# A fused block-sparse attention and gMLP kernel: first batch in two query halves, loads and weights reordered

## Chip, cores and metric

One core of a Trainium2 chip. The metric is the device time of one execution in microseconds (us). The kernel before takes 223.69 us, the median of 6 runs (223.38 to 223.85). All times within an execution are read from one profiled execution.

## The reference, cut to what matters

Four batches, 8 heads, 768 positions, head size 64. Attention with a block mask (blocks of 32: the neighbours, the first and last block row and column, and three sampled blocks per row), then a gated MLP with a spatial product over the positions.

```python
scores = np.where(mask, scale * q @ k.T, -1e9)          # per batch and head, 768 x 768
attn = softmax(scores);  x = concat_heads(attn @ v)      # x: 4 x 768 x 512
h = relu(x @ w_in);  u, v = h[..., :512], h[..., 512:]   # w_in: 512 x 1024
v_n = (v - mean(v)) / sqrt(var(v) + 1e-6)
v_s = einsum('ts,bsd->btd', w_spatial, v_n) + b_spatial  # w_spatial: 768 x 768
out = (u * v_s) @ w_out                                  # w_out: 512 x 512
```

## The kernel before, in words

The order of all instructions is written out by hand, and each engine executes its own in that order. Heads come in pairs: pair p holds two heads, four pairs make a batch, and there are 16 pairs. The main loop (L483 on) runs over p and 12 steps s; a step is called a slot here and numbered g = 12p + s, so that a batch has 48 slots and a head six.

A slot holds these parts:

- qk_exp (L285): two matmuls of 384 columns on TensorE (PE) give one 128-row chunk of keys against all 768 queries, in one of two PSUM tiles (ps, tag sc). ScalarE (ACT) takes their exponential (L294) into the tile a_all. The mask is added by the same matmul: rows 64 to 87 of the tiles kt and qt hold 24 block indicators and mask values. These tiles are filled once for head slot 0 and copied on VectorE (DVE) to slots 1 to 3 (mask_rows, L260 to 262); head j uses slot j % 4.
- av (L299), seven slots behind: six matmuls of 65 columns for a chunk of 128 queries. After six chunks, norm (L313) divides by the row sums (reciprocal L319, product L320) into xn. When both heads of a pair are done, xn is transposed to xt, by PE (L323) or by a DMA (L343).
- Matmuls of the gMLP of the batch before. moe_units (L362) makes 108 of them for a batch, each of 512 columns (L386): 48 for h, 36 for the spatial product, 24 for the output. They are added in slot 56 of the batch that follows and drawn from slot 57 on, spread over 48 slots. In the h part the order is v0 v1 v2 u0 v3 u1 v4 u2 v5 u3 u4 u5 (row chunks of the v and u halves; four matmuls each). A chunk of v gets its relu and statistics on DVE (on ACT in the last batch), and after three of them GpSimd (POOL) computes rstd (L403, L405). A chunk of u gets its relu on ACT (L415) and issues the normalization of the chunk of v before it (L409). The last batch's gMLP mostly runs after all attention.

The loads of q, k and v (L91) go through SyncE's queue (SP) into fp32 tiles st_q, st_k and st_v of two buffers each. POOL casts them to bf16 (prepare, L116; cast_v, L111; L109 and L112). Heads 0 and 1 are cast by halves, by DVE and ACT, and transposed one by one (tr_head, L225; copies L220). Pairs 1 to 5 are transposed by PE (tr_pair, L234, with DVE copies L244), later ones by DMA (tr_dma, L271, then split_pair, L276). PE's transposes and the gMLP share two PSUM buffers of tag moe. The weights are loaded in nine pieces (L138) into fp32 staging tiles that borrow buffers of gMLP tiles, and cast on POOL (L150): w_in in slots 7 and 19, w_spatial in slot 55, w_out in slot 79. w_spatial is transposed by six DMAs in slots 60 to 78 (wspt, L348). Loops over keep_warm (L178) are matmuls without use, at the start.

Of the kernel before, what the change touches and what calls it, by code (L numbers as in the profile page):

```python
# [26 lines left out]
def kernel(  # L27
# [16 lines left out]
    nc = tc.nc  # L44
# [29 lines left out]
    b_col = const.tile([128, NCH], FP32)  # L74
    mhalf = const.tile([128, NCH], FP32)

    qt = [const.tile([KR, S], BF16, name=f"qt{s}") for s in range(4)]
    kt = [const.tile([KR, S], BF16, name=f"kt{s}") for s in range(4)]
    vv = [const.tile([128, 2, NCH, VA], BF16, name=f"vv{s}") for s in range(3)]


    st = {}
# [1 line left out]
    def dram(src, b, h0, nh):  # L84
        return src[b, h0:h0 + nh].rearrange("h (p c) d -> p h (c d)", c=NCH)

    def st_tile(p, nm):
        st[nm, p] = work.tile([128, 2, NCH * D], FP32, tag=f"st_{nm}", bufs=2, name=f"st_{nm}")
        return st[nm, p]

    def load(p, names="qkv", eng=nc.sync):  # L91
        b, g = divmod(p, NG)
        for nm, src in (("q", q), ("k", k), ("v", v)):
            if nm in names:
                eng.dma_start(out=st_tile(p, nm), in_=dram(src, b, 2 * g, 2))

    nat = {}

    def nat_tile(p, nm):
        nat[nm, p] = work.tile([128, NCH, 2, D], BF16, tag=f"nat_{nm}", bufs=2,  # L100
                               name=f"nat_{nm}")
# [8 lines left out]

    def cast_v(p):  # L111
        nc.gpsimd.tensor_copy(  # L112
            out=vv[p % 3][:, :, :, 0:D],
            in_=st.pop(("v", p)).rearrange("p h (c d) -> p h c d", d=D))

    def prepare(p):  # L116
        for nm in "kq":
            nat_tile(p, nm)
            cast_qk(p, nm, slice(0, 2), nc.gpsimd)
        cast_v(p)  # L120

# [9 lines left out]
        w_pieces.append((moe_w_out.rearrange("(g p) f -> p g f", p=128)[:, 2 * g:2 * g + 2],  # L133
                         w_out_t[:, 2 * g:2 * g + 2, :]))
    w_staged = deque()
    w_tags = deque(["un", "vsb", "vn", "gn", "gt"])

    def load_weights(n):  # L138
        for _ in range(n):
# [19 lines left out]
    nc.sync.dma_start(out=samp_i, in_=_listify(sampled_blocks).bitcast(I32))  # L159
    for h in range(2):  # L160
        nc.sync.dma_start(out=stq[:, h:h + 1], in_=dram(q, 0, h, 1))
    load(0, "v", nc.sync)
    load(1, "qkv", nc.sync)
    nc.sync.dma_start(out=b_col, in_=moe_b_spatial.rearrange("(p c) -> p c", c=NCH))

    ind_nat = const.tile([NB, S], BF16)
    ind = const.tile([NB, S], BF16)
# [28 lines left out]
                            base=0, pattern=[[-1, NB], [0, BLK]], channel_multiplier=1)  # L196
    make_identity(nc, ident)

    for s in range(3):
        nc.gpsimd.memset(vv[s][:, :, :, D:VA], 1.0)  # L200
    nc.gpsimd.memset(mhalf, -0.5)

# [31 lines left out]
    def tr_pair(p, nm, third):  # L234
        if third == 0:
            tr_ps[nm] = psum.tile([128, S], BF16, tag="moe", bufs=2, name="ps_tr")
        src, ps = nat[nm, p], tr_ps[nm]
        for c in (2 * third, 2 * third + 1):
            nc.tensor.transpose(out=ps[:, c * 128:(c + 1) * 128],  # L239
                                in_=src[:, c].rearrange("p h d -> p (h d)"), identity=ident)  # L240
        if third == 2:
            nat.pop((nm, p))
            for h in range(2):
                nc.vector.tensor_copy(out=(qt if nm == "q" else kt)[(2 * p + h) % 4][0:D, :],  # L244
                                      in_=ps[h * D:(h + 1) * D, :])

    tr_head(0, "k", dve_copy)
# [9 lines left out]
    tr_head(0, "q", dve_copy)  # L257
    keep_warm(8, 128)

    def mask_rows(sl):  # L260
        nc.vector.tensor_copy(out=kt[sl][D:KR, :], in_=kt[0][D:KR, :])
        nc.vector.tensor_copy(out=qt[sl][D:KR, :], in_=qt[0][D:KR, :])

    def second_head():
        mask_rows(1)
        cast_qk(0, "k", slice(1, 2), nc.vector)
        cast_qk(0, "q", slice(1, 2), nc.vector)

    tt = {}

    def tr_dma(p, nm):  # L271
# [4 lines left out]
    def split_pair(p, nm):  # L276
        src = tt.pop((nm, p)).rearrange("x c n -> x (c n)")
        for h in range(2):
            nc.vector.tensor_copy(out=(qt if nm == "q" else kt)[(2 * p + h) % 4][0:D, :],  # L279
                                  in_=src[h * D:(h + 1) * D, :])  # L280


# [2 lines left out]
    def qk_exp(j, ci):  # L285
        if ci == 0:
            a_ref[j] = work.tile([128, NCH, S], BF16, tag="a_all", bufs=3, name="a_all")
        ps = psum.tile([128, 1024], FP32, tag="sc", bufs=2)
        for hf in range(2):
            nc.tensor.matmul(out=ps[:, hf * 512:hf * 512 + HALF],  # L290
                             lhsT=kt[j % 4][:, ci * 128:(ci + 1) * 128],
                             rhs=qt[j % 4][:, hf * HALF:(hf + 1) * HALF],
                             start=True, stop=True)
        nc.scalar.activation(  # L294
            out=a_ref[j][:, ci, :].rearrange("p (b c) -> p b c", b=2),
            in_=ps.rearrange("p (b c) -> p b c", b=2)[:, :, 0:HALF],
            func=AF.Exp, scale=0.125)

    def av(j, qc):  # L299
        if qc == 0:  # L300
            av_ref[j] = psum.tile([128, 512], FP32, tag="av", bufs=2,
                                  name="ps_av")[:, 0:NCH * VA].rearrange(
                                      "p (c d) -> p c d", d=VA)
        p, h = divmod(j, 2)
        for ci in range(NCH):
            nc.tensor.matmul(out=av_ref[j][:, qc, :],  # L306
                             lhsT=a_ref[j][:, ci, qc * 128:(qc + 1) * 128],
                             rhs=vv[p % 3][:, h, ci, :],
                             start=(ci == 0), stop=(ci == NCH - 1))
        if qc == NCH - 1:  # L310
            a_ref.pop(j)

    def norm(j):  # L313
        p, h = divmod(j, 2)
# [47 lines left out]
    def moe_units(b):  # L362
# [3 lines left out]
        vsb = work.tile([128, NCH, DH], BF16, tag="vsb", bufs=2)  # L366
        vn = work.tile([128, NCH, DH], BF16, tag="vn", bufs=2)
        gn = work.tile([128, NCH, DH], BF16, tag="gn", bufs=2)
        gt = work.tile([128, NCH, NDH, 128], BF16, tag="gt", bufs=2)
        mv = work.tile([128, NCH, 2], FP32, tag="mv", bufs=2)  # L370
        std = work.tile([128, NCH], FP32, tag="std", bufs=2)
        rstd = work.tile([128, NCH], FP32, tag="rstd", bufs=2)
# [48 lines left out]
        def in_proj(tcc, cols, post):  # L421
            add(NDM, lambda g: (xt(g)[:, tcc * 128:(tcc + 1) * 128], w_in_t[:, g, cols]),
                lambda ps: post(tcc, ps))

        for i in range(NCH + 2):
            if i < NCH:
                in_proj(i, slice(DH, DFF), v_post)
            if i >= 2:
                in_proj(i - 2, slice(0, DH), u_post)

        def g_tr(tcc):
            ps = psum.tile([128, S], BF16, tag="moe", bufs=2, name="ps_g")
# [39 lines left out]
    slots_left = 0  # L472
    LAG = 7

    for p in range(NP + 1):
        for s in range(12):
            g = 12 * p + s
            j, ci = divmod(g, NCH)
            if p == NP and g - LAG >= 2 * NP * NCH:
                break  # L480
            if p < NP:
                qk_exp(j, ci)
            if p == 0 and s == 0:  # L483
                second_head()
            if p == 0 and s < 6:
                keep_warm(2, 128)
            if p == 0 and s == 3:
                tr_head(1, "k", dve_copy)
            if p == 0 and s == 4:
                tr_head(1, "q", dve_copy)  # L490
                mask_rows(2)
                mask_rows(3)
            if p <= NG:
                first = 0 if p else 6
                if first <= s < first + 3:
                    tr_pair(p + 1, "k", s - first)
                elif first + 3 <= s < first + 6:
                    tr_pair(p + 1, "q", s - first - 3)
            elif p + 1 < NP and s in (5, 9):
                split_pair(p + 1, "k" if s == 5 else "q")  # L500
            if s == 10 and NG + 1 < p + 2 < NP:
                tr_dma(p + 2, "k")
                tr_dma(p + 2, "q")
            if p == 0 and s == 0:
                cast_v(0)
                prepare(1)
                load(2)
                load_weights(2)
            if s == 7 and p + 2 < NP:
                if p + 3 < NP:  # L510
                    load(p + 3)
                if p in (0, 3, 4, 5):
                    load_weights((2, 0, 0, 2, 1, 2)[p])
                prepare(p + 2)
                if p in (0, 1, 4, 6):
                    cast_weights((2, 2, 0, 0, 3, 0, 2)[p])
            if moe_q and slots_left > 0:
                budget += len(moe_q) / slots_left
                slots_left -= 1
                while moe_q and budget >= 0.5:  # L520
                    moe_q.popleft()()
                    budget -= 1
            if g >= LAG:
                ja, qc = divmod(g - LAG, NCH)
                av(ja, qc)
                if qc == NCH - 1:
                    norm(ja)
            if p in (NG + 1, NG + 2) and s in (0, 3, 6):
                wspt(3 * (p - NG - 1) + s // 3)
            if 1 <= p < NG and 8 <= s < 11:  # L530
                xtr_third(p - 1, s - 8)
            if s == 8 and p >= NG:
                xtr(p - 1)
                if p % NG == 0:
                    moe_q.extend(moe_units(p // NG - 1))
                    slots_left = 48 if p < NP - NG else 52
                    budget = 0.0
# [34 lines left out]
```

The softmax here doesn't subtract the row's maximum and nothing guards it: scores larger than these inputs give would overflow.

## Time and profile before

| | |
|---|---|
| median of 6 runs | 223.69 us |
| the profiled execution | 223.13 us |
| its span, first to last instruction | 221.4 us |
| PE busy | 214.2 us (97%) |
| ACT busy | 177.1 us (80%) |
| DVE busy | 128.2 us (58%) |
| POOL busy | 64.1 us (29%) |
| the 192 exps (L294), one | 814 ns |
| mean granted TensorE clock | 0.997 |

The span is shorter than the execution's time by what lies around the program. "a<-b" names the tile written and those read. The mean duration of an instruction is longer than its share of an engine's time where the next one begins before it ends; the distance between starts is then the cost. A note such as [0.42 <-PE ps L290] says that the engine was idle for 0.42 us until that instruction of PE was done. A q after an engine's name is its queue.

### The profile page before, as it was taken

The numbers are of one execution on the slowest core, as the hardware profiler recorded it, in microseconds if no ns is written. First come the engines' busy times: TensorE is split into PE (matmuls) and PEld (weight loads), VectorE is DVE, ScalarE is ACT, GpSimd is POOL, SyncE is SP. The second block draws the span as 40 slices with busy tenths as digits, with TensorE's granted clock in tenths as the row PEclk, the third lists the DMA queues.
The fourth block names the chain that finished last, engine by engine and source line by source line (L and its number), as shares of the span: only waits on it lengthen the run. The fifth ranks groups of instructions, "written<-read, shape, count | busy, mean of one in ns | idle before, by whom it ended". The sixth has DMA issues, their size and how long they took to land.

```text
span 221.4 us, 5325 instructions
## 1 busy us (share of the span) xinstructions
PE 214.2 (97%) x2154; PEld 129.8 (59%) x2154; DVE 128.2 (58%) x282; ACT 177.1 (80%) x246; POOL 64.1 (29%) x88
## 2 busy tenths in 40 slices
PE   7999999999999999999999999999999999999993
PEld 3567777676565656566565656566656665544541
DVE  5656445467868455368777544378674433676531
ACT  5699999998899888888899878888989884265351
POOL 5436770439905701210607101210501000022000
PEclk9999999999999999999999999999999999999998
DMA  6779999995899877999674397998141114610015
GB/s 193 234 278 384 387 307 332 340 142 64 254 280 135 263 106 210 196 316 277 209 172 144 78 104 225 180 318 244 30 80 36 38 40 89 229 73 0 0 61 225
DMA packets 56092, 40.25 MB, mean 182 GB/s; under 512 B 39300, under 2 KB 51588, under 8 KB 56068
## 3 DMA queue, kind: packets, MB, share of 16 engines
q1 hardware_dynamic: 55780, 39.53, 68.1%
q10 hardware_dynamic: 288, 0.39, 0.6%
q8 instruction: 16, 0.26, 0.5%
q14 instruction: 8, 0.07, 0.1%
HBM read 24.38 MB, written 6.29 MB: 139 GB/s over the span
## 4 chain that ended last, share of the span: by engine, by line
PE 81%; ACT 14%; DVE 2%; issue 1%; POOLq 0%; POOL 0%
PE ps_moe L386 31%; PE ps L290 23%; ACT a_all L294 13%; PE ps_av L306 13%; PE ps_t L386 6%; PE ps_sc L386 3%; PE wps L180 2%; PE ps L228 1%; PE ps_x L330 1%; PE ps_g L434 1%; POOLq L567 0%; DVE gn L441 0%; DVE stats L399 0%; PE ps_tr L239 0%; ACT vsb L394 0%
## 5 line engine op out<-in xcount | busy, mean ns | idle before, releaser
L294 ACT ACTIVATE a_all<-ps 128x768 bf16<-128x768 f32 x192 | 149.5, 814 | 19.3 <-PE ps L290 10.7
L290 PE MATMUL ps<-qt,kt 88*128 88x384 bf16 x384 | 93.7, 325 | 1.8 <-ACT a_all L294 0.6
L306 PEld LDWEIGHTS <-a_all 128*128 128x128 bf16 x1152 | 60.4, 97 | 37.0 <-issue 0.4
L306 PE MATMUL ps_av<-vv,a_all 128*128 128x65 bf16 x1152 | 67.9, 194 | 0.0
L386 PE MATMUL ps_moe<-w_in_t,xt 128*128 128x512 bf16 x144 | 42.1, 378 | 0.0
L386 PE MATMUL ps_moe<-vn,w_spt 128*128 128x512 bf16 x108 | 31.8, 379 | 0.0
L290 PEld LDWEIGHTS <-kt 88*128 88x128 bf16 x384 | 28.2, 97 | 4.7 <-issue 1.9
L386 PEld LDWEIGHTS <-xt 128*128 128x128 bf16 x192 | 18.6, 97 | 16.1 <-issue 0.3
L112 POOL CAST vv<-st_v 128x768 bf16<-128x768 f32 x16 | 13.4, 837 | 45.8 <-PE ps_av L306 42.6
L441 DVE SCALAR_TENSOR_TENSOR gn<-ps_moe,b_col,un 128x512 bf16<-128x512 f32 x18 | 13.5, 749 | 18.6 <-PE ps_moe L386 18.5
L403 POOL TENSOR_SCALAR std<-mv 128x3 f32<-128x3 f32 x8 | 2.2, 278 | 72.2 <-DVE mv L400 59.5
L386 PE MATMUL ps_moe<-w_out_t,gt 128*128 128x512 bf16 x72 | 20.6, 379 | 0.1
L386 PEld LDWEIGHTS <-w_spt 128*128 128x128 bf16 x144 | 13.7, 97 | 11.4 <-issue 0.9
L399 DVE BATCH_NORM_STATS2 stats<-vsb 128x6 f32<-128x512 bf16 x24 | 16.7, 694 | 3.3 <-ACT vsb L394 2.7
L320 DVE TENSOR_TENSOR xn<-ps_av,rc 128x384 bf16<-128x384 f32 x32 | 17.8, 558 | 1.1
L396 DVE TENSOR_SCALAR vsb<-ps_moe 128x512 bf16<-128x512 f32 x18 | 12.4, 690 | 10.3 <-PE ps_moe L386 10.3
L109 POOL CAST nat_k<-st_k 128x768 bf16<-128x768 f32 x15 | 12.4, 824 | 17.5 <-DMA st_k<-in_k_dram 8.8
L319 DVE RECIPROCAL rc<-ps_av 128x6 f32<-128x6 f32 x32 | 6.0, 188 | 15.7 <-PE ps_av L306 15.6
L386 PEld LDWEIGHTS <-gt 128*128 128x128 bf16 x96 | 8.8, 97 | 6.9
L109 POOL CAST nat_q<-st_q 128x768 bf16<-128x768 f32 x15 | 12.5, 833 | 0.0
L279 DVE COPY kt<-tt_k 64x768 bf16<-64x768 bf16 x20 | 8.5, 424 | 6.2 <-DMA tt_k<-nat_k 6.0
L409 DVE TENSOR_SCALAR vn<-vsb,mv,rstd 128x512 bf16<-128x512 bf16 x24 | 10.3, 447 | 2.6 <-POOL rstd L405 2.5
(80 smaller groups left out, 172.4 us busy)
## 6 DMA issues: line engine op xcount, KB each, us to landing
st_v<-in_v_dram SPq DMA_DIRECT2D x16, 384.0 KB, 5.7
out_dram<-osb SPq DMA_DIRECT2D x24, 256.0 KB, 2.6
st_q<-in_q_dram SPq DMA_DIRECT2D x15, 384.0 KB, 3.7
st_k<-in_k_dram SPq DMA_DIRECT2D x15, 384.0 KB, 4.7
wst<-in_moe_w_spatial_dram SPq DMA_DIRECT2D x3, 768.0 KB, 8.2
wst<-in_moe_w_in_dram SPq DMA_DIRECT2D x4, 512.0 KB, 8.5
wst<-in_moe_w_out_dram SPq DMA_DIRECT2D x2, 512.0 KB, 6.9
st_k<-in_k_dram ACTq DMA_DIRECT2D x2, 192.0 KB, 3.0
```

The costliest lines, as they stand in the source:

```text
L109: eng.tensor_copy(out=dst, in_=src)
L112: nc.gpsimd.tensor_copy(out=vv[p % 3][:, :, :, 0:D], in_=st.pop(("v", p)).rearrange("p h (c d) -> p h c d", d=D))
L279: nc.vector.tensor_copy(out=(qt if nm == "q" else kt)[(2 * p + h) % 4][0:D, :], in_=src[h * D:(h + 1) * D, :])
L290: nc.tensor.matmul(out=ps[:, hf * 512:hf * 512 + HALF], lhsT=kt[j % 4][:, ci * 128:(ci + 1) * 128], rhs=qt[j % 4][:, hf * HALF:(hf + 1) * ...
L294: nc.scalar.activation(out=a_ref[j][:, ci, :].rearrange("p (b c) -> p b c", b=2), in_=ps.rearrange("p (b c) -> p b c", b=2)[:, :, 0:HALF], ...
L306: nc.tensor.matmul(out=av_ref[j][:, qc, :], lhsT=a_ref[j][:, ci, qc * 128:(qc + 1) * 128], rhs=vv[p % 3][:, h, ci, :], start=(ci == 0), st ...
L320: nc.vector.tensor_tensor(out=xn_ref[p][:, :, h, :], in0=ps[:, :, 0:D], in1=rc.to_broadcast([128, NCH, D]), op=ALU.mult)
L386: nc.tensor.matmul(out=box[0], lhsT=lhs, rhs=rhs, start=(i == 0), stop=(i == n - 1))
L396: nc.vector.tensor_scalar(out=vsb[:, tcc, :], in0=ps, scalar1=0.0, scalar2=None, op0=ALU.max)
L399: nc.vector.bn_stats(out=stats, in_=vsb[:, tcc, :])
L409: nc.vector.tensor_scalar(out=vn[:, tcc, :], in0=vsb[:, tcc, :], scalar1=mv[:, tcc, 0:1], scalar2=rstd[:, tcc:tcc + 1], op0=ALU.subtract, ...
L441: nc.vector.scalar_tensor_tensor(out=gn[:, tcc, :], in0=ps, scalar=b_col[:, tcc:tcc + 1], in1=un[:, tcc, :], op0=ALU.add, op1=ALU.mult)
```

## The change

The first batch gets a loop of its own of 48 slots. It goes over all eight heads for queries 0 to 383, three slots a head, and then over them again for queries 384 to 767. A slot computes two chunks of keys for 384 queries (qk_exp_half) and one chunk of queries of av_half, four slots behind. xtr_half transposes half a pair's xn on PE. There are eight head slots of kt and qt, in one tile each; head j uses slot j % 8. The mask rows are copied by DVE to slots 1 to 3 and by two DMAs to slots 4 to 7. Loads are issued in the order k1 q1 v0 k2 q2 v1, the mask rows, k3 q3 v2, two pieces of w_in, v3, two pieces of w_in. vv has four buffers, gt one.

Batch 0's first 16 gMLP matmuls (v0 v1 u0 v2) are drawn in slots 31 to 34 and 43 to 46, two in each; the other 92 from slot 55 on over 50 slots. w_spatial is loaded in slot 8 and cast in slots 34 and 38, and transposed in slots 45 to 55. The order of v and u chunks differs by batch. The core of the diff:

```diff
-    qt = [const.tile([KR, S], BF16, name=f"qt{s}") for s in range(4)]
-    kt = [const.tile([KR, S], BF16, name=f"kt{s}") for s in range(4)]
-    vv = [const.tile([128, 2, NCH, VA], BF16, name=f"vv{s}") for s in range(3)]
+    qt_all = const.tile([KR, H, S], BF16)
+    kt_all = const.tile([KR, H, S], BF16)
+    qt = [qt_all[:, h] for h in range(H)]
+    kt = [kt_all[:, h] for h in range(H)]
+    vv = [const.tile([128, 2, NCH, VA], BF16, name=f"vv{s}") for s in range(NG)]
...
-    load(0, "v", nc.sync)
-    load(1, "qkv", nc.sync)
-    nc.sync.dma_start(out=b_col, in_=moe_b_spatial.rearrange("(p c) -> p c", c=NCH))
+    load(1, "kq")
+    load(0, "v")
...
+    def qk_exp_half(g):
+        gh, i = divmod(g, NCH // 2)
+        grp, j = divmod(gh, H)
...
+        ps = psum.tile([128, 1024], FP32, tag="sc", bufs=2)
+        for u in range(2):
+            ci = 2 * i + u
+            nc.tensor.matmul(out=ps[:, u * 512:u * 512 + HALF],
+                             lhsT=kt[j][:, ci * 128:(ci + 1) * 128],
+                             rhs=qt[j][:, grp * HALF:(grp + 1) * HALF],
+                             start=True, stop=True)
+        nc.scalar.activation(out=a_ref["half", gh][:, 2 * i:2 * i + 2, :],
+                             in_=ps.rearrange("p (b c) -> p b c", b=2)[:, :, 0:HALF],
+                             func=AF.Exp, scale=0.125)
...
-        gt = work.tile([128, NCH, NDH, 128], BF16, tag="gt", bufs=2)
+        gt = work.tile([128, NCH, NDH, 128], BF16, tag="gt", bufs=1)
...
+        order = ("v0 v1 u0 v2 u1 u2 v3 v4 u3 v5 u4 u5" if b == 0 else
+                 "v0 v1 v2 v3 v4 v5 u0 u1 u2 u3 u4 u5" if last else
+                 "v0 v1 u0 v2 u1 v3 u2 v4 u3 v5 u4 u5")
...
+    LAG0 = 4
+    N0 = H * NCH
+
+    cast_qk(0, "k", slice(1, 2), nc.vector)
+    cast_qk(0, "q", slice(1, 2), nc.scalar)
+    prepare(1, "kq")
+    cast_v(0)
+    def mask_rows(h):
+        for t in (kt, qt):
+            nc.vector.tensor_copy(out=t[h][D:KR, :], in_=t[0][D:KR, :])
+
+    mask_rows(1)
+    load(2, "kq")
+    load(1, "v")
+    for t in (kt_all, qt_all):
+        nc.sync.dma_start(out=t[D:KR, 4:H, :],
+                          in_=t[D:KR, 0:1, :].to_broadcast([NB, H - 4, S]))
+    load(3, "kq")
+    load(2, "v")
+    load_weights(2)
+    load(3, "v")
+    load_weights(2)
+    nc.sync.dma_start(out=b_col, in_=moe_b_spatial.rearrange("(p c) -> p c", c=NCH))
+
+    tr_slots = {}
+    for p, slots in ((1, (2, 2, 2, 3, 3, 3)), (2, (7, 8, 8, 9, 10, 10)),
+                     (3, (13, 14, 14, 15, 16, 16)), (4, (36, 37, 38, 39, 40, 41))):
+        for i, g in enumerate(slots):
+            tr_slots.setdefault(g, []).append((p, "kq"[i // 3], i % 3))
...
+    for g in range(N0):
+        qk_exp_half(g)
+        if g < 6:
+            keep_warm(2, 128)
+        if g < 2:
+            tr_head(1, "kq"[g], dve_copy)
+        for p, nm, third in tr_slots.get(g, ()):
+            tr_pair(p, nm, third)
+        if g in (1, 4):
+            mask_rows(2 if g == 1 else 3)
+        if g == 3:
+            prepare(2, "kq")
+            cast_v(1)
+        if g == 8:
+            prepare(3, "kq")
+            cast_v(2)
+            cast_v(3)
+            load(4, "kqv")
+            load_weights(3)
+        if g == 18:
+            cast_weights(4)
+            prepare(4, "kq")
+            load(5, "kq")
+        if g == 34:
+            prepare(4, "v")
+            load(5, "v")
+            cast_weights(2)
+        if g == 38:
+            prepare(5, "kq")
+            cast_weights(1)
+        if g == 43:
+            load(6, "kq")
+            prepare(5, "v")
+            load(6, "v")
+        if g == 45:
+            wspt(0)
+            wspt(1)
+        if g == 30:
+            moe_q.extend(moe_units(0))
+        if g in (31, 32, 33, 34, 43, 44, 45, 46):
+            moe_q.popleft()()
+            moe_q.popleft()()
+        first_batch_rest(g)
+
+    for p in range(NG, NP + 1):
...
+            if g == N0 + 7:
+                slots_left = 50
...
+            if p == NG and s in (2, 3, 6, 7):
+                wspt((2, 3, 6, 7).index(s) + 2)
```

## The prediction

> **What bounds the kernel now.** I read the stage windows first: busy time of each engine in equal stretches (the first pair of columns is the stretch and its length).
>
> ```profile
> core 0: us, PE busy (x) PEld busy (x) DVE busy (x) ACT busy (x) POOL busy (x), PEclk, DMA share, GB/s
> 24.00:32.00 8.00, 7.89 (x107) 5.92 (x106) 4.29 (x9) 8.00 (x12) 5.81 (x8) 1.00 0.96 327
> 88.00:96.00 8.00, 8.00 (x84) 4.80 (x82) 3.12 (x8) 7.14 (x11) 1.99 (x3) 1.00 1.08 224
> ```
>
> In the first batch ACT has no idle time; in the later batches PE has none. PE looks full in both rows, so the busy share doesn't separate them. The starts of PE's instructions do: first a slot of the first batch, then one with two gMLP matmuls.
>
> ```profile
> 39.55 0.48 PE L290 MATMUL ps<-qt,kt 88*128 88x384 bf16 x2
> 39.87 0.36 PE L306 MATMUL ps_av<-vv,a_all 128*128 128x65 bf16 x6
> 40.06 0.27 PE L330 MATMUL ps_x<-ident,xn 128*128 128x128 bf16 x2
> 40.25 0.48 PE L290 MATMUL ps<-qt,kt 88*128 88x384 bf16 x2
> ...
> 53.05 0.35 PE L306 MATMUL ps_av<-vv,a_all 128*128 128x65 bf16 x6
> 53.24 0.49 PE L290 MATMUL ps<-qt,kt 88*128 88x384 bf16 x2
> 53.57 0.60 PE L386 MATMUL ps_moe<-w_in_t,xt 128*128 128x512 bf16 x2
> 54.00 0.35 PE L306 MATMUL ps_av<-vv,a_all 128*128 128x65 bf16 x6
> ```
>
> A slot's QK takes 0.32-0.33 us of issue, its AV 0.19, together 0.52; two gMLP matmuls take 0.43, so 0.2165 each. With two of them a slot is 0.95. In the first batch the next QK starts 0.70 after the last: it waits for an exp, and about 0.18 us of PE per slot is free. ACT's timeline gives the first batch's exact length.
>
> ```profile
> 7.87 2.92 ACT L294 ACTIVATE a_all<-ps 128x768 bf16<-128x768 f32 x4 [1.02 <-PE ps L290]
> 10.95 0.81 ACT L294 ACTIVATE a_all<-ps 128x768 bf16<-128x768 f32 x1 [0.17 <-PE ps L290]
> 11.95 5.04 ACT L294 ACTIVATE a_all<-ps 128x768 bf16<-128x768 f32 x7 [0.19 <-PE ps L290]
> 17.41 25.61 ACT L294 ACTIVATE a_all<-ps 128x768 bf16<-128x768 f32 x36 [0.42 <-PE ps L290]
> 43.24 8.26 ACT L294 ACTIVATE a_all<-ps 128x768 bf16<-128x768 f32 x11 [0.23 <-PE ps_av L306]
> ```
>
> Counting the x's, exp 0 starts at 7.87 and exp 48 (second batch) at 43.24: 35.37 us for 48. Their pitch is 0.70 (2.92 less the last one's 0.81, over 3), plus about 0.07 at each change of the a_all tile: 34.0 without stalls, so some 1.3 us is lost. From slot 57, at 49.74, to the end PE is the bound, without a gap worth naming until the tail.
>
> **The change, part by part.**
>
> *Sixteen of batch 0's 108 gMLP matmuls move into the first batch.* Later, on a full PE, that removes 16 x 0.2165 = 3.46 us. In addition they begin at slot 55, not 57. Before, slots 48 to 56 lasted 49.74 - 43.24 = 6.50. After, slots 48 to 54 last 7 x 0.70 + 0.07 = 4.97, and 55 and 56 add only their own 2 x 0.52 of PE work to the full stage: 6.01, or 0.49 less. Against that, 1.84 matmuls per slot replace 2.25, so a slot is 0.52 + 0.40 = 0.92 and ACT's relus (0.60 at L415, before an exp) get closer to being late; I allow 0.2. Sum: -3.75.
>
> *The same sixteen in the first batch are not free.* They come two per slot, in two runs of four slots. A slot grows from 0.70 to 0.95; four make 1.0 more, and only the first can draw on slack (an exp's input lies ready about 0.15 us early): 0.83 per run. The second run also puts u0's relu (0.60) on ACT, which the stalls of PE largely cover: 0.2. Sum: +1.85. Bounds: 1.2 (ACT a whole slot ahead) and 2.6 (relu fully exposed).
>
> *Query halves.* QK, exp and AV keep their number and size per slot (two 384-column matmuls, one 768-column exp, six AV matmuls). Reciprocals and normalizations double in number at half size, on a DVE busy 4.3 of 8 us there. The transposes of x are as many as before. Slots with four transposes (8, 10, 14, 16) reach 0.52 + 0.22 = 0.74: +0.25 with those of slots 0 to 2.
>
> *What is needed earlier.* Head 1 is due at slot 3 instead of 6, head 2 at 6 instead of 12, head 4 at 12 instead of 24. The price is in DVE's queue: the second half of k0's cast, the mask rows of head 1, the two transposed copies of head 1, then the mask rows of head 2 and the copies of heads 2 and 3. PE waits behind it: the transposes of pair 1 wait for a PSUM buffer that the kt copy of head 1 frees, and QK of slot 3 stands behind them and needs the qt copy. Here the trace shows what a mask row costs beside a cast.
>
> ```profile
> 7.30 0.35 DVE L261 COPY kt<-kt 24x768 bf16<-24x768 bf16 x1
> 7.38 0.97 POOL L112 CAST vv<-st_v 128x768 bf16<-128x768 f32 x1 [3.24 <-DMA st_v<-in_v_dram]
> 7.58 0.97 DVE L262 COPY qt<-qt 24x768 bf16<-24x768 bf16 x1
> ```
>
> The first copy, begun before the cast, took 0.35; the second, begun inside it, 0.97, and ended 0.20 after the cast. The Trainium skill (SBUF — State Buffer, "Who interferes with whom") says why: a VectorE copy in a two-port mode and a GpSimd operation lock one port pair for a whole instruction. It speaks against this change, which puts k1's and q1's casts (landings at about 7.3 and 8.3, the times at which v0 and q1 come now) beside these copies. By the uncontended row, the DVE queue is k0b to 7.6, masks to 8.2, kt copy to 9.05 and qt copy (0.55 each, L220) to 9.65: QK 3 at 9.7, exp 3 at 10.2 against an ideal 9.97, a loss of 0.3. By the lock: the k mask ends at 8.55 behind k1's cast, the q mask at 9.5 behind q1's, the copies at 10.05 and 10.6: QK 3 at 10.7, exp 3 at 11.2, a loss of 1.25. I take the lock: at 68.2-70.1, two casts following each other let in just one DVE operation between them (0.90 and 0.97 instead of 0.38 and 0.35). Later copies and masks add 0.25 by slot 9. Start: +1.5, bounds 0.4 and 2.6.
>
> *Loads.* Each st buffer is taken over from the pair before, so k2 waits on SP for POOL's cast of k1 (8.3), q2 for q1's (9.3), and v1, the two mask DMAs, k3, q3 and v2 stand behind. The trace's st_q issued at 10.99 needed 3.4 us to land, with about 1.02 per 384 KB behind it. So k2 lands at 11.8, q2 12.8, v1 13.9, k3 15.7, q3 16.8, v2 17.8, v3 21.6. With slots at 9.4 + 0.70 n, each is cast (0.83) before its use: pair 2's transposes from slot 7 (14.3), v1 at 10 (16.4), pair 3 from 13 (18.5), v2 at 16, v3 at 22 (24.8). The cover is 1 to 2 us; past it every microsecond counts whole. The mask DMAs have no row: 147 KB each is 0.4 us at the 380 GB/s seen, and a few engines could stretch it to over 6. The skill (DMA: Bandwidth & Descriptors, "Why a DMA increments its semaphore by 16 and not by 1") lets 24 rows use 12 of 16 engines: an estimate of 0.5, which I take; slot 12 needs them at 17.9, and they land near 15. Nothing.
>
> *Weights.* w_in's casts (1.04 x 4) end near 27, before slot 31 at 31.4. Spatial's three (8.77 together) run beside first-batch DVE operations that read PSUM; those keep their times beside casts in the trace (L220 at 0.55 both ways). The six spatial transposes come forward on SP, in front of pair 7's loads and tt of pair 6, which then lands near 60 for slot 65 at about 59. DVE already waits 3.4 us for a tt once without a PE gap. Nothing, at worst +1. The extra vv buffer and single gt hide behind whole stages.
>
> *Order in gMLP.* In the last batch all v precede all u.
>
> ```profile
> 203.01 1.06 DVE L409 TENSOR_SCALAR vn<-vsb,mv,rstd 128x512 bf16<-128x512 bf16 x3 [1.09 <-POOL rstd L405]
> 203.48 1.02 PE L386 MATMUL ps_sc<-vn,w_spt 128*128 128x512 bf16 x3 [0.20 <-DVE vn L409]
> ```
>
> The first six spatial matmuls run from 202.47 to 204.34, 1.87 instead of 1.30, since v5's statistics are late. With 24 matmuls of u (5.2 us) over the 3.2 us of statistics, they are not: -0.57. In other batches u1 directly follows v2; DVE then waits about 1.3 us for rstd, ahead of its next job. Nothing.
>
> Sum: first batch 34.0 + 1.5 + 0.25 + 1.85 = 37.6 against 35.37, +2.2; after it -3.75 - 0.57 = -4.3. Net -2.1: a span of 219.3, a profiled execution of 221.0 instead of 223.13, and from the median 223.69 (the profiled one is 0.56 below) 221.6.
>
> **Rivals.** *The start is cheap:* if the copies slip between the casts (0.4, not 1.5), 220.5. For: the first copy did; against: the casts now queue up. Chance 0.22. *The freed PE time is not all recovered:* ACT's relus, tt late, or a run costing its upper bound eat 1 to 2: 223.0. Chance 0.2, half within 0.2%. *The mask DMA is the new wait:* place, slot 12; price, one microsecond for each that both land after 17.9, with k3 and q3 queued behind. On one engine (1/16 of 380 GB/s) two times 147 KB take 12 us, so slot 12 starts 9 late: about 230. It decides from 2.5 us late, 20.4. For: no row shows such a DMA; against: the 12-engine rule. Chance 0.1, slower.
>
> **How the numbers follow.** Forecast 0.48 (220.9 to 222.4), start cheap 0.22, partly recovered 0.2, mask DMA 0.1. About 0.2% (0.45 us) can be told from no change. Faster: 0.48 + 0.22 + 0.09 = 0.79; same 0.09; slower 0.02 + 0.1 = 0.12. The range 220.2 to 223.4 takes in the first three but for half of the partly recovered and some of the cheap start's end.
>
> **What would show it.** Exp 3 near 11.2 (10.2: the lock doesn't bite); exp 48 near 45.5; two runs of four slots at 0.95 around 32 and 42; from slot 55 slots of 0.92; no pause at the first spatial matmuls of the tail. I am wrong if exp 12 starts after 19.5, if PE shows gaps after slot 55, or if exp 48 comes before 44.

## The result and the profile after

The changed kernel takes 225.34 us, the median of 16 runs (224.22 to 228.66); the kernel before, run beside it, 223.53 us (35 runs). The ratio is 1.0084, 95% interval 1.0065 to 1.0102: slower by 0.8%, where 0.9% less was forecast. The profiled execution took 226.5 us with a span of 224.7 us. A second run of the same kernel (e1_again) gave 1.0065 [1.0038, 1.0092] and a span of 223.1 us. Some executions fall in a slower state; the ratios leave them out, the medians take in all.

The forecast was made in stages, so the result is read in stages: from the start of one exp to that of another, by ACT's timeline, here of the changed kernel (start, busy time, instruction, count, and the idle time before it with its releaser).

```profile
9.57 0.81 ACT L322 ACTIVATE a_all<-ps 128x768 bf16<-128x768 f32 x1 [1.37 <-PE ps L318]
10.89 0.81 ACT L322 ACTIVATE a_all<-ps 128x768 bf16<-128x768 f32 x1 [0.50 <-PE ps L318]
11.88 7.46 ACT L322 ACTIVATE a_all<-ps 128x768 bf16<-128x768 f32 x10 [0.18 <-PE ps L318]
19.66 1.51 ACT L322 ACTIVATE a_all<-ps 128x768 bf16<-128x768 f32 x2 [0.32 <-PE ps L318]
21.66 23.52 ACT L322 ACTIVATE a_all<-ps 128x768 bf16<-128x768 f32 x31 [0.49 <-PE ps L318]
...
45.56 2.48 ACT L322 ACTIVATE a_all<-ps 128x768 bf16<-128x768 f32 x3
47.98 4.33 ACT L287 ACTIVATE a_all<-ps 128x768 bf16<-128x768 f32 x6
```

L322 is the exp of the first batch, L287 that of the others. Counting the x's, exp 12 starts at 19.66 (1 + 1 + 10 before it; the forecast's limit was 19.5), exp 14 at 21.66, and exp 48 at 47.98, 48 exps in all before it. Where a row ends and the next begins with a gap, as after exps 0, 1, 11 and 13, ACT stalled. The table holds such differences, in us, for the kernels that matter; a row sums to its span. e2_order to e9_own_only are variants, told below. The forecast's row is worked out from its own steps.

| | exp 0 starts | 0 to 6 | 6 to 24 | 24 to 48 | 48 to 104 | 104 to 144 | 144 to 191 | 191 to last matmul | rest | span |
|---|---|---|---|---|---|---|---|---|---|---|
| before | 7.87 | 4.79 | 13.26 | 17.33 | 53.84 | 40.69 | 46.17 | 33.55 | 3.86 | 221.4 |
| forecast | 7.87 | - | - | - | 50.09 | 40.69 | 46.17 | 32.98 | 3.86 | 219.3 |
| after | 9.57 | 5.42 | 13.99 | 18.99 | 49.95 | 42.32 | 46.18 | 32.97 | 5.32 | 224.7 |
| e1_again | 8.15 | 5.47 | 14.99 | 19.00 | 49.94 | 42.33 | 46.18 | 32.97 | 4.05 | 223.1 |
| e2_order | 7.82 | 5.66 | 14.92 | 18.99 | 51.00 | 41.14 | 46.18 | 32.97 | 4.04 | 222.7 |
| e3_vv3 | 9.58 | 5.65 | 13.12 | 19.00 | 49.94 | 42.73 | 46.18 | 32.98 | 4.05 | 223.2 |
| e9_own_only | 9.58 | 5.54 | 13.12 | 19.00 | 49.94 | 42.32 | 46.18 | 32.97 | 4.05 | 222.7 |
| e6_own | 7.59 | 5.43 | 13.12 | 18.99 | 49.94 | 40.94 | 46.18 | 32.97 | 4.06 | 219.2 |

The forecast's first batch, exp 0 to 48, was 37.6; it is 39.46 in the repetition and 38.40 in the first profile. So against 219.3 the repetition's 223.1 is +1.9 in the first batch, +1.6 between exp 104 and 144, +0.3 before exp 0 and +0.2 at the end. What the change was to gain is there: 48 to 104 takes 3.9 less than before, the tail 0.58 less. It is given back in two places.

The first profile's exp 0 at 9.57 and its rest of 5.32 vary between executions: the repetition, the same instructions, has 8.15 and 4.05. What differs at the start is PE's pace, here in the same six transposes of q0, in the changed kernel and in e1_again:

```profile
7.08 0.85 PE L230 MATMUL ps<-ident,nat_q 128*64 128x128 bf16 x6
```

```profile
6.45 0.52 PE L230 MATMUL ps<-ident,nat_q 128*64 128x128 bf16 x6
```

Four of the eleven profiles of kernels that start as the changed one does have exp 0 at 9.57 or 9.58, and none of the three that start as the kernel before (7.87 to 8.36). That is too few to say whether the change makes the late start more frequent. It matters for what follows, since the loads don't wait for exp 0. The changed kernel, e1_again, e2_order, e3_vv3 and e5_nomove have the same first 24 slots and loads, and yet take 19.41, 20.46, 20.58, 18.77 and 19.28 from exp 0 to exp 24; the forecast's terms give 18.75 (half of 34.0, and 1.5 and 0.25). Their k3 lands between 17.97 and 19.79, and with a late start it is late by less.

*First place: slot 12 and slots around it.* The chain of work that ended last, in the changed kernel (start, length, what); its longest piece is one transfer, the mask rows of qt:

```profile
10.68 8.33 DMA qt_all<-qt_all
19.00 0.14 issue
19.14 0.48 PE ps L318 x2
```

Issued at 10.68, landed at 19.0, and QK of slot 12 (the first use of head slot 4) starts 0.14 later. After it the chain runs over POOL's cast of k3, at 19.94: k3 landed at 19.8. In e1_again PE waits for two loads there, for the cast of v1 before slot 12 and for that of k3 before slot 14:

```profile
17.62 0.35 PE L334 MATMUL ps_av<-vv,a_all 128*128 128x65 bf16 x6 [0.75 <-POOL vv L113]
20.45 0.28 PE L241 MATMUL ps_tr<-ident,nat_k 128*128 128x128 bf16 x2 [0.70 <-POOL nat_k L110]
```

*Second place: at about 122 us.* DVE, POOL and PE of the changed kernel, in order of time, at v5 of batch 1:

```profile
121.24 0.95 POOL L113 CAST vv<-st_v 128x768 bf16<-128x768 f32 x1
122.13 0.95 POOL L110 CAST nat_k<-st_k 128x768 bf16<-128x768 f32 x1
122.41 1.64 DVE L454 TENSOR_SCALAR vn<-vsb,mv,rstd 128x512 bf16<-128x512 bf16 x2
123.28 0.38 PE L431 MATMUL ps_moe<-vn,w_spt 128*128 128x512 bf16 x1 [0.86 <-DVE vn L454]
124.11 0.38 PE L431 MATMUL ps_moe<-vn,w_spt 128*128 128x512 bf16 x1 [0.45 <-DVE vn L454]
```

PE, the bound here, idles 0.86 and 0.45 for vn. In the kernel before, at the same place:

```profile
119.16 0.73 DVE L409 TENSOR_SCALAR vn<-vsb,mv,rstd 128x512 bf16<-128x512 bf16 x2
```

There the two vn take 0.73 together: POOL is idle for the 1.59 us before its next cast, at 120.16. No PE gap follows.

### The profile page after: what moved, and what is told of

Same layout as the page of the kernel before. It is cut to its first block, busy times and chain, and to the rows that moved or that the text cites. A ratio compares the mean times of both kernels' runs of the same rounds, so it can differ in the third digit from the quotient of the medians.

```text
span 224.7 us, 5351 instructions
## 1 busy us (share of the span) xinstructions
PE 214.9 (96%) x2154; PEld 129.6 (58%) x2154; DVE 133.2 (59%) x301; ACT 178.0 (79%) x247; POOL 64.0 (28%) x89
## 4 chain that ended last, share of the span: by engine, by line
PE 83%; ACT 5%; DVE 4%; DMA 4%; POOL 1%; issue 1%; SPq 0%; POOLq 0%; ACTq 0%
PE ps_moe L431 30%; PE ps L283 19%; PE ps_av L299 12%; PE ps_t L431 7%; PE ps L318 5%; DMA qt_all<-qt_all 4%; PE ps_sc L431 3%; ACT a_all L322 3%; PE ps_av L334 2%; PE wps L182 2%; ACT a_all L287 2%; DVE vn L454 1%; DVE kt_all L272 1%; PE ps L230 1%; PE ps_tr L241 1%
## 5 line engine op out<-in xcount | busy, mean ns | idle before, releaser
L287 ACT ACTIVATE a_all<-ps 128x768 bf16<-128x768 f32 x144 | 114.3, 813 | 16.3 <-PE ps L283 8.2
L283 PE MATMUL ps<-qt_all,kt_all 88*128 88x384 bf16 x288 | 70.3, 325 | 0.3 <-ACT a_all L287 0.2
L431 PE MATMUL ps_moe<-w_in_t,xt 128*128 128x512 bf16 x144 | 42.7, 378 | 0.0
L322 ACT ACTIVATE a_all<-ps 128x768 bf16<-128x768 f32 x48 | 35.7, 814 | 3.8 <-PE ps L318 2.9
L431 PE MATMUL ps_moe<-vn,w_spt 128*128 128x512 bf16 x108 | 32.5, 378 | 1.3 <-DVE vn L454 1.3
L318 PE MATMUL ps<-qt_all,kt_all 88*128 88x384 bf16 x96 | 23.8, 329 | 0.9 <-ACT a_all L322 0.2
L283 PEld LDWEIGHTS <-kt_all 88*128 88x128 bf16 x288 | 19.3, 98 | 0.9 <-issue 0.7
L444 DVE BATCH_NORM_STATS2 stats<-vsb 128x6 f32<-128x512 bf16 x24 | 16.7, 695 | 1.4 <-ACT vsb L439 0.8
L454 DVE TENSOR_SCALAR vn<-vsb,mv,rstd 128x512 bf16<-128x512 bf16 x24 | 12.9, 567 | 4.6 <-POOL rstd L450 4.5
L365 DVE TENSOR_TENSOR xn<-ps_av,rc 128x384 bf16<-128x384 f32 x24 | 13.4, 557 | 0.8
```

The lines of the kernel that those rows point to most:

```text
L283: nc.tensor.matmul(out=ps[:, hf * 512:hf * 512 + HALF], lhsT=kt[j % H][:, ci * 128:(ci + 1) * 128], rhs=qt[j % H][:, hf * HALF:(hf + 1) * ...
L287: nc.scalar.activation(out=a_ref[j][:, ci, :].rearrange("p (b c) -> p b c", b=2), in_=ps.rearrange("p (b c) -> p b c", b=2)[:, :, 0:HALF], ...
L318: nc.tensor.matmul(out=ps[:, u * 512:u * 512 + HALF], lhsT=kt[j][:, ci * 128:(ci + 1) * 128], rhs=qt[j][:, grp * HALF:(grp + 1) * HALF], s ...
L322: nc.scalar.activation(out=a_ref["half", gh][:, 2 * i:2 * i + 2, :], in_=ps.rearrange("p (b c) -> p b c", b=2)[:, :, 0:HALF], func=AF.Exp, ...
L365: nc.vector.tensor_tensor(out=xn_ref[p][:, :, h, :], in0=ps[:, :, 0:D], in1=rc.to_broadcast([128, NCH, D]), op=ALU.mult)
L431: nc.tensor.matmul(out=box[0], lhsT=lhs, rhs=rhs, start=(i == 0), stop=(i == n - 1))
```

## Experiments

Theory: the loss has two causes that add up, the loads of the first batch (their cover is used up) and the order of v and u in batches 0 to 2 (v5 too late). Rivals: the fourth vv buffer moves POOL's casts and so makes the later gap; the mask DMAs alone make the first loss; the sixteen moved matmuls cost more than they bring.

**The changed kernel once more**, for the spread between executions.

> The changed kernel once more, for a second profile. Two theories. First: three waits cost the forecast gain: the mask DMAs (slots 12 to 14), the normalization of v chunks 4 and 5 at the start of batch 1's spatial product (1.3 us of PE gaps at 122 to 124 us), and the early start; the late first exp (9.57 instead of 7.87 us) and the late last store (1.4 us) of the first profile are chance. Then a second profile has exp 0 near 7.9, exp 48 minus exp 0 near 38.4, and the same gaps at slot 129; the time is 225.3. Second: the late first exp and the late last store belong to the change; then both show again.

1.0065 [1.0038, 1.0092]. The gaps and the landings recur. Exp 0 at 9.57 doesn't, nor the long end.

**The order alone taken back.** On the changed kernel:

```diff
-                 "v0 v1 u0 v2 u1 v3 u2 v4 u3 v5 u4 u5")
+                 "v0 v1 v2 u0 v3 u1 v4 u2 v5 u3 u4 u5")
```

> The changed kernel with the middle batches' order of v and u chunks as in the kernel before (v0 v1 v2 u0 v3 u1 v4 u2 v5 u3 u4 u5). First theory: twelve matmuls instead of eight stand between v5 and the spatial product, 1.7 us more for its statistics: the gaps at slot 129 are gone or below 0.3, 1.3 to 1.6 less than the changed kernel, 223.8. Second theory (the start and the end): 225.3, the same as the changed kernel.

0.9995 [0.9973, 1.0017]. 104 to 144 falls from 42.33 to 41.14, and PE has no gap at v5 of batch 1. POOL's casts still follow each other there, and the two vn take as long as in the changed kernel:

```profile
121.43 1.64 DVE L454 TENSOR_SCALAR vn<-vsb,mv,rstd 128x512 bf16<-128x512 bf16 x2
```

So the order of before doesn't shorten what DVE does; it leaves the time to cover it. In this profile 1.06 is lost between 48 and 104 that the changed kernel didn't lose there (PE gaps of 0.91 and 0.36 near 88 and 99 us, behind DVE, which waited 3.2 us for a transposed tt_k). e6_own has the same edit and doesn't show it.

**Three vv buffers instead of four, from pair 4 on:**

```diff
-            out=vv[p % NG][:, :, :, 0:D],
+            out=vv[p if p < NG else (p - NG) % 3][:, :, :, 0:D],
```

(and the same index where av reads it).

> The changed kernel with three vv buffers in turn from pair 4 on, as in the kernel before, so that POOL's casts of v wait for AV and two pairs' casts don't follow each other at once. First theory: the six casts in a row at 119.6 to 124.7 us, which hold up DVE's normalizations, part; the gaps at slot 129 shrink to half or less: 224.3 (bounds 223.7 to 225.0). If the order alone makes the gaps: 225.3.

1.0045 [1.0018, 1.0072]; the six casts still follow each other, the two gaps stay, at 0.87 and 0.45 us, and 104 to 144 is 42.73. The fourth vv buffer isn't what makes them.

**The order alone put into the kernel before**, first in the last batch, then in the batches 0 to 2:

```diff
+        order = ("v0 v1 v2 v3 v4 v5 u0 u1 u2 u3 u4 u5" if last else
+                 "v0 v1 v2 u0 v3 u1 v4 u2 v5 u3 u4 u5")
```

> The kernel before with the last batch's order alone (all v before all u). Theory: the tail is 0.57 shorter (33.55 to 32.98 from exp 191 to the last matmul), ratio 0.9974.

0.9972 [0.9952, 0.9992]; the tail goes from 33.55 to 32.98, the forecast's 0.57.

```diff
+        order = ("v0 v1 v2 u0 v3 u1 v4 u2 v5 u3 u4 u5" if last else
+                 "v0 v1 u0 v2 u1 v3 u2 v4 u3 v5 u4 u5")
```

> The kernel before with the changed order in batches 0 to 2 alone (v0 v1 u0 v2 u1 v3 and so on). Theory: v5's statistics come four matmuls later and DVE's normalizations meet POOL's casts: gaps at the spatial starts of batch 1, 1.0 to 1.6 us more between exps 104 and 144, ratio 1.005 to 1.008. Rival (only with the other parts of the change, its four vv buffers above all): 1.000.

1.022 [1.019, 1.0249], with nothing else of the change in it. Its profile, in batch 0:

```profile
72.86 2.20 POOL L153 CAST w_out_t<-wst 128x1024 bf16<-128x1024 f32 x2
73.14 2.07 DVE L409 TENSOR_SCALAR vn<-vsb,mv,rstd 128x512 bf16<-128x512 bf16 x2
74.22 0.38 PE L386 MATMUL ps_moe<-vn,w_spt 128*128 128x512 bf16 x1 [1.09 <-DVE vn L409]
```

Again two vn beside two casts that follow each other, and PE waits for each (1.09 here, 0.66 for the next). In batch 1 the gaps are 0.87 and 0.45. From 57 to 104 it is 49.57 against 47.35, from 104 to 144 42.35 against 40.69: together 3.9 of the 4.6 by which the profiled span (226.0) is longer. The order alone makes the later gap, then; in the changed kernel's batch 0 three vn run beside casts too (2.56 us from 67.44 on), but just early enough: PE has no gap there.

**A staging tile of their own for k2 and q2** (on e2_order), so that they need not wait for the casts of k1 and q1:

```diff
+        if p == 2 and nm in "kq":
+            if nm == "k":
+                st["own"] = work.tile([128, NCH * DH // 2], FP32, tag="gn", bufs=2,
+                                      name="st_own").rearrange("p (w h x) -> p w h x", w=2, h=2)
+            st[nm, p] = st["own"][:, "kq".index(nm)]
+            return st[nm, p]
```

> The changed kernel with the middle order of before; k2 and q2 get a staging tile of their own (a buffer of tag gn, free then), so that their loads wait for no cast. Theory: the DMA queue doesn't pause at 9 to 11 us, k2 and q2 land by 11.4, v1 and the mask rows about 2 us earlier, k3 by 17.5 instead of 19.4; exp 24 minus exp 0 falls from 20.5 to about 19, ratio to the kernel before 0.993. Rival (the mask DMAs alone slow the queue): exp 24 minus exp 0 falls by less than 0.5, ratio 0.998.

0.9934 [0.9911, 0.9957], 222.53 us: faster than both kernels. The load of k2 is issued at 3.62, not at 8.15 as in e1_again, that of q2 at 4.16, not 9.13. What the DMAs move is seen in windows of e1_again and then of e6_own (columns as in the forecast's first view; the last two are the DMA share and GB/s):

```profile
8.00:10.00 2.00, 1.84 (x20) 1.19 (x19) 1.94 (x4) 1.43 (x2) 1.70 (x3) 1.00 0.42 92
14.00:16.00 2.00, 1.79 (x27) 1.18 (x26) 1.54 (x5) 2.00 (x4) 0.83 (x1) 1.00 1.02 177
```

```profile
8.00:10.00 2.00, 2.00 (x27) 1.45 (x25) 1.56 (x5) 1.47 (x3) 1.45 (x2) 1.00 1.04 336
12.00:14.00 2.00, 1.64 (x26) 1.14 (x23) 1.89 (x6) 1.79 (x4) 0.36 (x1) 1.00 1.11 141
```

Two things are to be seen. In e1_again the DMA engines pause while k2 and q2 wait for POOL (92 GB/s at a share of 0.42); in e6_own they don't. In both there is also a stretch in which the share is full but only 141 to 177 GB/s are moved: there the mask DMAs run. The window of 14 to 16 of the kernel before, without such DMAs, moves 396 GB/s. With the staging tile v1 lands at 14.1 instead of 16.7, k3 at 16.5 instead of 19.4, q3 at 17.6 instead of 20.5, v3 at 22.8 instead of 25.1, and ACT shows what that is worth:

```profile
13.02 29.32 ACT L328 ACTIVATE a_all<-ps 128x768 bf16<-128x768 f32 x39 [0.21 <-PE ps L324]
```

From exp 6 on 39 exps follow each other; the stalls before 12 and 14 are gone. From exp 6 to 24 it is 13.12, where e1_again has 14.99. The profile alone would not prove it: e3_vv3, with a late start and no such tile, has 13.12 too. The timed runs decide, 0.9934 against e2_order's 0.9995.

**The staging tile on the changed kernel, its order of v and u kept:**

> The changed kernel with the staging tile for k2 and q2 and nothing else (its own order of v and u chunks). Theory: the two causes add up, so this is the middle-order kernel with that tile (ratio 0.9934) plus the gaps at slot 129 (1.4 us): ratio 0.9997, exp 24 minus exp 0 near 18.6, gaps of 0.87 and 0.45 again. Rival (they don't add up, since a first batch that ends earlier moves the casts away from the spatial product): 0.994.

0.9999 [0.9978, 1.0020], exp 0 to 48 in 37.65, and 104 to 144 in 42.32 with the gaps of 0.86 and 0.45. The 37.65 says little, since this profile started late and e3_vv3 has 37.77 without the tile. The timed runs say more: each cause can be repaired by itself, and each is worth 0.6 to 0.7% (e9_own_only against e1_again, and e6_own against e9_own_only).

**Mask rows 4 to 7 copied by DVE instead of the two DMAs**, on the changed kernel late (slots 7, 11, 13, 18), on e2_order early (5, 9, 11, 12):

```diff
-    for t in (kt_all, qt_all):
-        nc.sync.dma_start(out=t[D:KR, 4:H, :],
-                          in_=t[D:KR, 0:1, :].to_broadcast([NB, H - 4, S]))
...
-        if g in (1, 4):
-            mask_rows(2 if g == 1 else 3)
+        if g in (1, 4, 7, 11, 13, 18):
+            mask_rows({1: 2, 4: 3, 7: 4, 11: 5, 13: 6, 18: 7}[g])
```

> The changed kernel with the mask rows of head slots 4 to 7 copied by DVE (eight copies more, in slots 7, 11, 13 and 18) and without the two DMAs. First theory: k3 lands near 16 instead of 19.8 us, no wait at slots 12 and 14, exp 48 minus exp 0 falls from 38.4 to 37.3: 224.2. If the mask DMAs are covered, or the copies cost as much: 225.3.

1.0076 [1.0042, 1.0110], a miss. k3 does land earlier, at 16.9. But DVE's copies meet the casts of w_in:

```profile
24.90 4.25 POOL L156 CAST w_in_t<-wst 128x1024 bf16<-128x1024 f32 x4
26.08 1.18 DVE L532 COPY qt_all<-qt_all 24x768 bf16<-24x768 bf16 x1
```

The copy of qt takes 1.18, that of kt before it 0.83, instead of 0.35. ACT stalls for 0.63 us before slot 21, the first that needs them, and for 0.68 before slot 18.

> The changed kernel with the middle order of before; the mask rows of head slots 4 to 7 are copied by DVE in slots 5, 9, 11 and 12, ahead of w_in's casts, and the two mask DMAs are gone. Theory: k3 lands near 17 instead of 19.4 us, no wait at slots 12 to 15, exp 24 minus exp 0 falls from 20.5 to about 19.2, ratio to the kernel before 0.994. Rival (the wait for k2 and q2 is what counts, and DVE's copies cost what the DMAs did): above 20.2, ratio 0.999.

1.0024 [0.9999, 1.0049]. k3 lands at 15.7. Earlier copies avoid w_in's casts, but DVE is then late with xn (PE waits 0.91 us for it near slot 11), and exp 0 to 24 takes 20.61, as in e2_order (20.58). What is gained in the queue is lost on DVE.

**Staging tile and DVE copies together:**

> Both: the staging tile for k2 and q2, mask rows by DVE, and the middle order of before. Theory: the loads keep 1.02 us per 384 KB from the start, and only the queue of DVE beside POOL's casts is left: exp 24 minus exp 0 near 18.5, exp 48 minus exp 0 near 37.5, ratio to the kernel before 0.990. If loads aren't the cause of the slow first slots: as the better of the two.

1.0085 [1.0041, 1.0129], a miss: exp 0 to 24 in 21.00, against 18.55 with the tile alone, though k3 lands at 13.8. PE waits 0.76 and 1.29 us for DVE's copies and xn. The mask DMAs are the cheaper way once loads start early.

**No gMLP matmuls in the first batch** (e2_order without the drawing of sixteen in slots 31 to 46):

> The changed kernel with the middle order of before, and none of batch 0's gMLP matmuls in the first batch: all 108 are drawn from slot 55 on. Theory: the two runs of four slots cost 1.9 us of the first batch (exp 31 to 48 takes 12.3 instead of 14.2 us), and 16 x 0.2165 = 3.5 us come back in slots 57 to 104 (47.2 instead of 43.3 us): 1.5 us more than with the middle order alone, a ratio to the kernel before of 1.006. Rival (moving them is worth nothing, because the first batch pays in full): no difference, 0.9995.

1.0199 [1.0149, 1.0250]. In its profile the run of 31 to 48 takes 12.16 instead of 14.03, so the sixteen cost 1.87 there; 48 to 104 takes 55.55 instead of 51.00, more than expected (PE has gaps of 0.61 and 1.24 there). Moving them pays, and the third rival falls. Its profiled span is 223.7, and the timed runs (median 229.05) lie further above it than e2_order's do, for which I have no cause.

**The sixteen spread, one per slot in 31 to 46**, on e6_own, to use the 0.18 us of PE that a slot has free:

```diff
-        if g in (31, 32, 33, 34, 43, 44, 45, 46):
-            moe_q.popleft()()
+        if 31 <= g < 47:
             moe_q.popleft()()
```

> The middle-order kernel with the staging tile, and batch 0's 16 first matmuls drawn one per slot in slots 31 to 46 instead of two in each of eight. Theory: a slot of 0.52 + 0.22 = 0.74 is 0.04 over ACT's pitch, six with transposes 0.11 more, u0's relu up to 0.6: exp 31 to 48 takes 13.3 to 13.9 instead of 14.03; ratio 0.991 to 0.993. Rival (PE's free time per slot is less than 0.18, and single matmuls cost as much as pairs): 14.0 or more, 0.9934.

1.0080 [1.0055, 1.0106], a miss. Exp 36 to 43 takes 9.36 instead of 5.05:

```profile
43.43 0.34 PE L361 MATMUL ps_x<-ident,xn 128*128 128x128 bf16 x3 [0.81 <-DVE qt_all L252]
```

A chunk's four matmuls, spread over four slots, hold one of the two PSUM buffers of tag moe for that long; the transposes of pair 4 and of x share what is left, and PE waits until DVE has emptied it, 2.3 us in all in these seven slots. Two runs of four slots, placed around those transposes, are the better choice.

## Why the prediction was wrong

Step by step, with e1_again's numbers where the profiles differ.

- *Sixteen matmuls move* was right: 48 to 104 takes 49.94, 3.90 less than before, forecast 3.75.
- *The same sixteen in the first batch* was right: exp 31 to 48 takes 1.87 more in e2_order than in e5_nomove, forecast 1.85. PE's starts in the changed kernel show the slot of 0.95 (33.36, 34.30, 35.25):

```profile
33.36 0.48 PE L318 MATMUL ps<-qt_all,kt_all 88*128 88x384 bf16 x2
33.68 0.60 PE L431 MATMUL ps_moe<-w_in_t,xt 128*128 128x512 bf16 x2
...
34.30 0.49 PE L318 MATMUL ps<-qt_all,kt_all 88*128 88x384 bf16 x2
```

- *What is needed earlier* was right in size, and in mechanism for one of the two mask copies. Exp 3 starts 3.07 after exp 0, 3.33 in the forecast (11.2 less 7.87). The lock is seen in the changed kernel's first mask copies:

```profile
8.76 0.83 POOL L113 CAST vv<-st_v 128x768 bf16<-128x768 f32 x1 [0.15 <-DMA st_v<-in_v_dram]
8.85 0.95 DVE L532 COPY kt_all<-kt_all 24x768 bf16<-24x768 bf16 x1
9.72 0.34 DVE L532 COPY qt_all<-qt_all 24x768 bf16<-24x768 bf16 x1
```

0.95 inside a cast and 0.34 outside of one, as the Trainium skill has it (SBUF — State Buffer, "Who interferes with whom"). The cast was v0's, and q1's in e1_again, not k1's; the second copy met none, where the forecast had both behind casts.

- *Order in gMLP*, last batch: right, 0.58 less. The last vn start at 202.90, 2 us before the first six spatial matmuls, which now take 1.46 without a pause:

```profile
202.90 1.06 DVE L454 TENSOR_SCALAR vn<-vsb,mv,rstd 128x512 bf16<-128x512 bf16 x3 [0.46 <-POOL rstd L450]
204.94 1.46 PE L431 MATMUL ps_sc<-vn,w_spt 128*128 128x512 bf16 x6
```

- In the *other batches* "Nothing" was wrong, and this is one of the two failed steps: 104 to 144 takes 1.64 more. The forecast had seen that DVE would wait for rstd and stopped there. It did not ask how much time v5 has. In the new order v5 is one chunk later: eight matmuls of u, not twelve, lie between it and the spatial product; at some two a slot and 0.95 us a slot, it has about 1.9 us less. In that smaller cover DVE has two kt copies and two vn to do, and POOL's casts, which follow each other without a pause there, let in one DVE operation each: the two vn take 1.64 instead of 0.73. b2_mid shows the loss without the rest of the change, and e2_order takes it back by the order alone, with the two vn still at 1.64. Batch 2 is the counter-case: its v5 falls where POOL has no casts left, and 144 to 191 takes 46.18 in the new order and 46.17 in the old. So it takes both, the short cover and the casts; that the casts are the second is read from these rows, as no run takes them away alone.
- *Loads*, "Nothing", is the other failed step, worth 1.9 in e1_again's first batch. The forecast saw the waits and gave a cover of 1 to 2 us past which "every microsecond counts whole"; it sized what stands in the queue behind k2 too small. k2 landed at 11.3, forecast 11.8. From there to the landing of k3 the forecast had 3.9 (to 15.7), and e1_again took 8.1 (to 19.4). Four kernels part this sum. Here are POOL's casts of k2 and k3, each begun 0.15 after the landing, whatever releaser its note names: with the mask DMAs (e1_again) and without (e7_mask), then with the staging tile and the mask DMAs (e6_own) and with the tile alone (e8_both).

```profile
11.46 0.83 POOL L110 CAST nat_k<-st_k 128x768 bf16<-128x768 f32 x1 [1.19 <-DMA st_k<-in_k_dram]
19.57 0.83 POOL L110 CAST nat_k<-st_k 128x768 bf16<-128x768 f32 x1 [2.00 <-PE ps_av L334]
```

```profile
10.89 0.83 POOL L110 CAST nat_k<-st_k 128x768 bf16<-128x768 f32 x1 [0.99 <-PE ps L318]
15.88 0.83 POOL L110 CAST nat_k<-st_k 128x768 bf16<-128x768 f32 x1 [0.23 <-DMA st_k<-in_k_dram]
```

```profile
10.49 0.87 POOL L116 CAST nat_k<-st_own 128x768 bf16<-128x768 f32 x1 [0.29 <-PE ps L324]
16.69 0.83 POOL L116 CAST nat_k<-st_k 128x768 bf16<-128x768 f32 x1 [1.72 <-DMA st_k<-in_k_dram]
```

```profile
10.80 0.83 POOL L116 CAST nat_k<-st_own 128x768 bf16<-128x768 f32 x1
13.98 0.84 POOL L116 CAST nat_k<-st_k 128x768 bf16<-128x768 f32 x1 [0.32 <-DMA st_k<-in_k_dram]
```

The distances are 8.11, 4.99, 6.20 and 3.18. The two mask DMAs add 3.1 without the tile and 3.0 with it, about 1.5 each. The forecast had put them at 0.5 each by the skill's rule that 24 rows use 12 of 16 engines (DMA: Bandwidth & Descriptors, "Why a DMA increments its semaphore by 16 and not by 1"). The count of engines fits the trace: such a DMA's semaphore gets 13 updates and a load's 16, as twelve engines and one write for the four others would give. It is the rate that failed. While they run, the DMA share is full and the packets are slower, those of the loads too: 171 ns on average in the microsecond from 14 of e1_again, for the same 1536 bytes that take 65 in the loads of the kernel before.

The pause adds the other 1.8 to 1.9. The forecast had counted it up to k2's landing and let the later loads follow at 1.02 each. They did so in e8_both, where the queue never stood empty, and not in e7_mask; why is open. With 1.0 allowed for the mask DMAs, the two terms make 4.0 of the 4.2 by which k3 is later than forecast. Single executions spread, though: 6.96 to 9.11 over the five profiles with e1_again's loads, 5.37 in e4_maskdve for e7_mask's, 6.48 and 6.63 in e9_own_only and e10_spread for e6_own's. By the means the mask DMAs add some 3 and the pause 1.4 to 2. A load lands with the last of its 16 engines, and one can be far behind: in e1_again fifteen had k3 by 17.83.

The staging tile leaves the mask DMAs as they are, but k3 lands at 16.5, and the cover is enough again.

- *Query halves* held: from exp 24 to 31 it is 4.96 in e1_again and in e6_own, as in the kernel before. *Weights* held in the changed kernel, which has no PE gap for a tt; in e2_order a wait of DVE for a tt did cost PE 0.91.
- The rival *mask DMA is the new wait* had the right place: slot 12 did wait for it, and they landed at 19.0 in the first profile, 1.1 after the 17.9 from which they count and before the 20.4 from which they would make the kernel slower by themselves. The price of 9, one engine's, was too much by far. *The freed PE time is not all recovered* had the outcome closest to the result, by causes that it didn't name.

With both losses repaired (e6_own), the profiled span is 219.2, and the forecast was 219.3. That this is so close is partly luck: the profiled execution (221.01) lies 1.5 us below the median of its kernel (222.53), and its exp 0 starts 0.28 earlier than before. The ratio is 0.9934 [0.9911, 0.9957], where the forecast's 221.6 of 223.69 is 0.9907, so about seven tenths of the forecast gain are there, with a tile that the forecast didn't have. Open are a cheaper copy of the mask rows (none was found), whether the change makes the late start more frequent, and why the timed runs of e5_nomove and e8_both (medians 229.05 and 228.08) lie 3 to 4 us above their profiled executions.

## What to carry to other kernels

"Hidden by a cover of 1 to 2 us" is no zero: name what each late transfer adds, and subtract it from the cover in turn. Count a kind of transfer that no row shows at more than its bytes suggest, or measure it first, and ask what a queue loses when it stands empty because the next load waits for a buffer. When a chain is put later in an order, count what is left between its end and its first use, and look at which other engine's work falls into that stretch; the same 1.64 us of vn cost nothing at the spatial product of e2_order and 1.3 us of PE's time in the changed kernel. And when a change bundles gains and losses, a stage table finds the losses in one reading, and each can be taken away alone; more than one profile of each stage is needed where the start varies. e6_own keeps the gain of 48 to 104 and is the fastest of all.

## What the runs showed of the hardware

- A DMA that copies 24 rows from SBUF to four places in SBUF slows a whole queue: the same packets of 1536 bytes take 171 to 196 ns on average instead of 65, and the queue moves 141 to 177 GB/s at a full share, instead of 396. Two of them put off the landing of the load behind by about 3 us (3.0 from e8_both to e6_own, 3.1 from e7_mask to e1_again).
- Loads behind a pause of the queue came later than without one: from k2's landing to k3's 4.99 and 5.37 us in e7_mask and e4_maskdve, 3.18 in e8_both.
- GpSimd casts without a pause between them let in one VectorE operation each: the two vn 1.64 us instead of 0.73, with w_out's longer casts 2.07.
- The start of one and the same program varies: exp 0 starts at 9.57 in one profiled execution of the changed kernel and at 8.15 in the other, with six matmuls of 128 columns at 0.85 us near 7 us in the first and at 0.52 in the second. Over all kernels it lies between 7.50 and 9.58.
